# Scores of rounded units: the two heads of a pair in two halves of TensorE's rows, and queries rounded in one pass

## The chip, the cores and the metric

One core of a Trainium2 chip runs the kernel; seven stay idle. The metric is device time in microseconds of one execution, as the median of several runs. PE is TensorE (its weight loads are listed apart as PEld), DVE is VectorE, ACT ScalarE, POOL GpSimd, SP the engine that issues the DMAs.

## The reference

```python
B, H, S, D = 4, 8, 768, 48
for t in range(S):                       # a linear attention with decay, per head
    cur = u * kt (outer) vt
    y[:, :, t] = rt . (state + cur)
    state = wt * state + kt (outer) vt
x = y as (B * S, H * D) = (3072, 384)
x = elu(x @ w_in) @ w_out                # 384 -> 2048 -> 384
x = silu(x @ w2_in) @ w2_out             # 384 -> 2048 -> 384
```

All inputs and the output are float32.

## The kernel before

The attention is cut into 24 units: unit n is a chunk of L = 128 tokens of one batch (chunk n // 4, batch n % 4) with all 8 heads, as NP = 4 pairs. A pair lies in 112 partitions: its first head in rows 0 to 47 (padded to 64), its second in rows 64 to 111 (`HALF` names the two parts). For a unit, decays are built by scans on DVE, queries `tq` and keys `tk` are scaled with them, and within the chunk the output is a masked product of scores and values (`within`), outside of it a product with the state (`past`); `outer` and `update` bring the state on.

Scores are computed in one of two ways. Units 0 to 8 use plain float32: for each pair and head a matmul of the 64 or 48 rows of that head with 128 moving columns; the program issues each plain matmul as two passes, and the trace shows both. Units 9 to 23 (`n >= FIRST_ROUNDED`) use rounded float32: keys and queries are split into a high and a low part (`rounding`, lines 232 and 233: ACT copies to the rounded type, POOL subtracts), and three products, high by high, high by low, low by high, are added up in PSUM. There the queries are kept padded, `[112, 4, 2, 128]`, the first head's values in one of the two slots and zeros in the other rows (memset once, line 100), so that one matmul of all 112 rows and 256 moving columns gives the scores of both heads. A unit's scores come in two runs of six matmuls, `scores(0)` for pairs 0 and 1 and `scores(1)` for pairs 2 and 3, each into a PSUM bank of its own.

The two MLPs run in blocks of 512 tokens with all weights split in the same way into rounded high and low parts. A step f of the first MLP is `hidden` (line 443: nine matmuls of 512 columns), the activation (lines 450 to 459 on ACT and DVE), the split of its result (465 and 466) and, two steps later, `out_first` (line 474: nine matmuls). The second MLP is at lines 443 and 482.

The order is written out by hand. Units 0 to 3 run densely at the start; units 4 to 23 are threaded into the first MLP of the blocks before them. `slot` calls `tick` twice in each step f, once after `hidden` and once after `out_first`, and a tick takes the next of a unit's six parts (`round_ticks`). For unit n, with the preparation of unit n + 1 between its parts: t0 `scores(0)`, scan; t1 `scores(1)`, backward scan, `masked(0)`; t2 `masked(1)`, rounding of the queries of n + 1; t3 rounding of its keys; t4 nothing more for rounded units; t5 `past`, `outer`, `within` (lines 342, 316, 361), `ktok` of n + 1 (line 253: the keys transposed on PE, into the PSUM tile ktp), `update` (326, 328, 330), `split` (373, 374) and `ktok_copy` (line 259: ACT copies ktp away). Each engine works through its own instructions in the order of the program. In a block about four of five ticks take a part, so that between t5 and the next unit's t0 there are one or more groups of nine dense matmuls.

The PSUM tiles of scores, `ktp`, `upd`, `y` and the sums of unrounded units share one pool of three banks (`ps_a`). A tile that is allocated takes a bank that was used before, and its first writer waits until the last reader of that bank is done. `masked` (line 304) copies the scores above the diagonal on DVE into the attention tile `am`.

Of the kernel before, what the change touches and what calls it, by code (L numbers as in the profile page):

```python
# [7 lines left out]
F32 = mybir.dt.float32  # L8
F32R = mybir.dt.float32r
# [11 lines left out]
FIRST_ROUNDED = sum(BLOCKS[:2]) + 1  # L21
# [13 lines left out]
def kernel(  # L35
# [21 lines left out]
    nc = tc.nc  # L57
# [3 lines left out]
    RB = w_ch.shape[2]  # L61
    L = 128
    NCH = S // L
    NU = B * NCH
    NP = H // 2
# [24 lines left out]
    def rounded_open():  # L90
        staging.close()
        stage["x"] = attn.enter_context(tc.tile_pool(name="o1", bufs=1))
        stage["rk"] = attn.enter_context(tc.tile_pool(name="tok_rk", bufs=1))
        load_unit(SUMMED, "kr")
        p = attn.enter_context(tc.tile_pool(name="rounded", bufs=1))
        for i in "hl":
            rounded["k" + i] = p.tile([RB, NP, L], F32R, name="k" + i)

            q = rounded["q" + i] = p.tile([RB, NP, 2, L], F32R, name="q" + i)
            nc.gpsimd.memset(q.bitcast(F32), 0.0)  # L100

    x2_d = dram.tile([128, KT, NT], F32, name="x2_d")

# [2 lines left out]
    upper = const.tile([128, 128], I8, name="upper")  # L106
# [11 lines left out]
    rounded = {}  # L118
# [15 lines left out]
    HALF = (slice(0, 64), slice(64, RB))  # L134
# [5 lines left out]
    def load_unit(n, names):  # L140
        c, b = divmod(n, B)
        for nm in names if n < NU else "":
            if nm in "rk" and (n < SUMMED or "rk" not in stage):
                continue
            src, shape, pool, bufs = dict(
                w=(w_ch, [RB, W1 + 1], one_p, 2), c=(rk_ch, [RB, 2, NP, L], one_p, 2),
                r=(r_tok, [128, H * D], stage.get("rk"), 3), k=(k_tok, [128, H * D], stage.get("rk"), 3),
                v=(v_tok, [128, NP, 64 + D], tok_p, 2))[nm]
            t = un[n][nm] = pool.tile(shape, F32, tag="in_rk" if nm in "rk" else f"in_{nm}", name=f"in_{nm}", bufs=bufs)
            nc.sync.dma_start(t, src[b, c])  # L150

    def prep_steps(n):

        st = un[n]
# [76 lines left out]
        def rounding(x, hi, lo):  # L231
            nc.scalar.activation(out=hi, in_=x, func=ACTF.Copy)  # L232
            nc.gpsimd.tensor_tensor(out=lo, in0=x, in1=hi.bitcast(F32), op=ALU.subtract)  # L233

        def q():
            tq = st["q"] = ch_p.tile([RB, NP, L], F32, tag="tq", name="tq")
            nc.vector.tensor_tensor(out=tq, in0=st["c"][:, 0], in1=st["g4"][:, :, 0:L], op=ALU.mult)
            if n >= FIRST_ROUNDED:
                for e, rows in enumerate(HALF):
                    rounding(tq[rows], *(rounded["q" + i][rows, :, e, :] for i in "hl"))  # L240

        def kt():
            tk = st["kd"] = ch_p.tile([RB, NP, L], F32, tag="tk", name="tk")
# [11 lines left out]
        def ktok_copy():  # L255
            if n // B == NCH - 1:
# [3 lines left out]

        return dict(ktok=ktok, ktok_copy=ktok_copy, scan=scan, scan_back=scan_back, far=far, whole_decay=whole_decay, bonus=bonus, products=products, summed=summed, diag=diag,
                    q=q, kt=kt)


# [4 lines left out]
    def pe_steps(n, xt, col, free=None):  # L269
        ch, b = divmod(n, B)  # L270
        st = un[n]
        ps = {}

        def ps_att(shape, name):
            if free and name == "sc":
                return free.pop(0).rearrange("p (j t) -> p j t", j=NP)
            return ps_a.tile(shape, F32, tag="att", name=name)


        def scores(h):  # L280
            if n < FIRST_ROUNDED:

                if h == 0:
                    ps["p"] = [ps_att([128, NP, L], "sc") for _ in range(2)]
                for j in (2 * h, 2 * h + 1):
                    for e, rows in enumerate(HALF):
                        nc.tensor.matmul(
                            ps["p"][e][:, j, :], st["kd"][rows, j, :], st["q"][rows, j, :], start=True, stop=True)
                return
            p = ps["p", h] = ps_att([128, 2, 2, L], "sc")  # L290
            terms = [(rounded["k" + a], rounded["q" + b]) for a, b in ("hh", "hl", "lh")]
            for jj in range(2):
                j = 2 * h + jj
                for i, (a, b) in enumerate(terms):
                    nc.tensor.matmul(  # L295
                        p[:, jj].rearrange("p e t -> p (e t)"), a[:, j, :],
                        b[:, j].rearrange("p e t -> p (e t)"), start=i == 0, stop=i == len(terms) - 1)

        def masked(h):
            if n < FIRST_ROUNDED:  # L300
                to, p = st["a"][:, :, h, :], ps["p"][h]
            else:
                to, p = (t.rearrange("p j e t -> p (j e) t") for t in (st["a"][:, 2 * h:2 * h + 2], ps["p", h]))
            nc.vector.copy_predicated(to, upper.unsqueeze(1).to_broadcast([128, NP, L]), p)  # L304

        last = ch == NCH - 1

        def outer():
            if last:
                return  # L310
            p = ps["u"] = ps_att([RB, NP, D], "upd")
            for j in range(NP):

                for c in range(0, RB, 32):
                    rows, e = slice(c, min(c + 32, RB)), c // 64
                    nc.tensor.matmul(  # L316
                        p[rows, j, :], st["kt"][:, j, rows], st["v"][:, j, 64 * e:64 * e + D],
                        start=True, stop=True)

        def update():  # L320
            if last:
                return
            s, up = packed[b], ps["u"]
            g = st["gl"].to_broadcast([RB, NP, D])
            if ch:
                nc.vector.tensor_tensor(out=s, in0=up, in1=s, op=ALU.add)
                up = s
            nc.vector.tensor_tensor(out=s, in0=up, in1=g, op=ALU.mult)
            for e, rows in enumerate(HEAD):
                nc.scalar.activation(out=state[b][rows, :, e * D:(e + 1) * D], in_=s[rows], func=ACTF.Copy)  # L330

        def past():

            y = ps["y"] = ps_att([128, KT, L], "y")
            if not ch:
                return
            for kt in range(KT):
                for base in range(4):  # L340
                    j, i = divmod(4 * kt + base, 3)
                    nc.tensor.matmul(  # L342
                        y[32 * base:32 * base + 32, kt, :], state[b][:, j, 32 * i:32 * i + 32], st["q"][:, j, :],
                        start=kt == 0, stop=False, skip_group_check=True)

        def within():
            y = ps["y"]
            vf = st["v"].rearrange("p j c -> p (j c)")
            for step in range(4):
                for base in range(4):  # L350


                    todo = []
                    for kt in range(KT):
                        blk = 4 * kt + base
                        j, i = divmod(blk, 3)
                        ha, hb = (64 + D) * j, (64 + D) * j + 64
                        todo += {0: [(blk, 2 * j, ha)], 1: [(blk, 2 * j, ha + 32), (blk, 2 * j + 1, hb - 16)],
                                 2: [(blk, 2 * j + 1, hb + 16)]}[i]
                    blk, h, c = todo[step]  # L360
                    nc.tensor.matmul(  # L361
                        y[32 * base:32 * base + 32, blk // 4, :], vf[:, c:c + 32], st["a"][:, h // 2, h % 2, :],
                        start=not ch and step == 0, stop=step == 3 or todo[step + 1][0] != blk,
                        skip_group_check=True)

        def split():
            split_x(xt, slice(col, col + L), ps["y"], nc.vector)

        return dict(scores=scores, masked=masked, outer=outer,
                    update=update, past=past, within=within, split=split)  # L370

    def split_x(xt, sl, src, eng):
        nc.scalar.activation(out=xt["h"][:, :, sl], in_=src, func=ACTF.Copy)
        eng.tensor_tensor(
            out=xt["l"][:, :, sl], in0=src, in1=xt["h"].bitcast(F32)[:, :, sl], op=ALU.subtract)
# [356 lines left out]
    with tc.manual_schedule():  # L732
# [25 lines left out]
        for j, units in enumerate(BLOCKS):  # L758
# [38 lines left out]
            if j == 0:  # L797
                assert not halves and not whole
                rounded_open()
# [192 lines left out]
```

## Time and profile before

| | us |
|---|---|
| median of 3 runs (lowest, highest) | 949.76 (948.05, 950.05) |
| the profiled execution | 947.38 |
| its span on the core | 945.6 |
| PE busy in the span | 918.1 |
| DVE, ACT, POOL busy | 489.4, 502.4, 133.9 |

The profile is of one execution, which is not one of the three runs of the median. Busy shares are averages; what counts for a stage is which engine the others wait for in it. The duration that a matmul has in the trace is modelled and overlaps the next one, so distances between the starts of matmuls tell more than their durations. In a row of the timeline the numbers are the start in microseconds from the start of the span and the duration.

### The profile page before, as it was taken

To read this page: it belongs to the slowest core of one execution; us is meant where nothing else is said; L and a number is where in the kernel's file an instruction comes from. 1 tells how busy PE (TensorE), PEld (TensorE's weight loads), DVE (VectorE), ACT (ScalarE), POOL (GpSimd) and SP (SyncE) were. 2 spreads that over 40 slices of the span, in tenths; PEclk is the share of its full clock that TensorE was granted. 3 is DMA by queue.
4 is the path that set the end of the run, shared out by engine and by line. 5 is a ranking of instruction groups with operands and counts; after the bars stand their busy time and mean duration, and the time that the engine had idled before them with its cause. 6 is when DMAs were issued, how large, how long until landed. Compare 5 with 4: busy or idle time off the path is not lost.

```text
span 945.6 us, 15205 instructions
## 1 busy us (share of the span) xinstructions
PE 918.1 (97%) x6158; PEld 790.8 (84%) x6158; DVE 489.4 (52%) x726; ACT 502.4 (53%) x901; POOL 133.9 (14%) x101
## 2 busy tenths in 40 slices
PE   7779899999999999999999999999999999999996
PEld 7667688888888888888888899999999999999996
DVE  7798877776666776666378762212212212222211
ACT  6788866665655655555488963323323333333332
POOL 0000012443453334453000000000000000000000
PEclk8799999999999999999999999999999999999998
DMA  8644414222322221220245330100200200200001
GB/s 252 184 153 161 163 48 124 69 67 57 110 67 73 91 66 57 78 68 1 101 141 193 136 99 1 67 0 1 68 1 1 68 1 1 67 1 1 34 1 37
DMA packets 32222, 68.69 MB, mean 73 GB/s; under 512 B 3600, under 2 KB 13968, under 8 KB 32144
## 3 DMA queue, kind: packets, MB, share of 16 engines
q1 hardware_dynamic: 32144, 67.64, 22.5%
q8 instruction: 50, 0.82, 0.4%
q14 instruction: 28, 0.23, 0.1%
HBM read 58.19 MB, written 9.44 MB: 72 GB/s over the span
## 4 chain that ended last, share of the span: by engine, by line
PE 89%; DVE 6%; DMA 2%; ACT 2%; issue 1%; SPq 0%; DVEq 0%; ACTq 0%
PE ph L443 40%; PE po L482 21%; PE po L474 19%; PE sc L295 2%; PE y L361 2%; PE y L342 1%; DVE wst L414 1%; PE ktp L253 1%; DVE wl L429 1%; DVE wst L416 1%; DMA in_v<-in_v_tok_dram 1%; DVE am L304 1%; DVE gl L466 1%; PE upd L316 1%; DMA above_sb<-in_above_dram 1%
## 5 line engine op out<-in xcount | busy, mean ns | idle before, releaser
L466 DVE TENSOR_TENSOR gl<-g,gh 128x512 fp32r<-128x512 f32 x192 | 144.8, 754 | 313.5 <-ACT gh L465 313.3
L443 PE MATMUL ph<-xh,wh 128*128 128x512 f32 x576 | 227.6, 395 | 2.1 <-DVE g L459 2.1
L443 PE MATMUL ph<-xh,wl 128*128 128x512 f32 x576 | 227.4, 395 | 0.0
L443 PE MATMUL ph<-xl,wh 128*128 128x512 f32 x576 | 227.2, 394 | 0.0
L465 ACT ACTIVATE gh<-g 128x512 fp32r<-128x512 f32 x192 | 120.8, 629 | 153.7 <-PE po L482 109.7
L454 ACT ACTIVATE g<-ph 128x512 f32<-128x512 f32 x96 | 57.4, 598 | 137.8 <-PE ph L443 137.1
L482 PE MATMUL po<-wh,gl 128*128 128x384 f32 x384 | 129.5, 337 | 0.0
L482 PE MATMUL po<-wh,gh 128*128 128x384 f32 x384 | 129.3, 337 | 0.0
L482 PE MATMUL po<-wl,gh 128*128 128x384 f32 x384 | 128.9, 336 | 0.0
L443 PEld LDWEIGHTS ph<-xh,wl 128*128 128x128 f32 x576 | 108.7, 189 | 23.5
L443 PEld LDWEIGHTS ph<-xh,wh 128*128 128x128 f32 x576 | 109.1, 189 | 22.4 <-DVE g L459 2.5
L443 PEld LDWEIGHTS ph<-xl,wh 128*128 128x128 f32 x576 | 108.8, 189 | 19.5
L474 PE MATMUL po<-gh,wh 128*128 128x512 f32 x288 | 114.7, 398 | 0.0
L474 PE MATMUL po<-gl,wh 128*128 128x512 f32 x288 | 113.0, 392 | 0.0
L474 PE MATMUL po<-gh,wl 128*128 128x512 f32 x288 | 112.7, 391 | 0.0
L450 ACT ACTIVATE g<-ph 128x512 f32<-128x512 f32 x96 | 56.5, 589 | 52.2 <-PE ph L443 52.1
L459 DVE SCALAR_TENSOR_TENSOR g<-g,ph 128x512 f32<-128x512 f32 x96 | 65.4, 681 | 27.7 <-ACT g L452 27.1
L482 PEld LDWEIGHTS po<-wh,gh 128*128 128x128 f32 x384 | 72.2, 188 | 4.3 <-ACT x2s L493 0.2
L482 PEld LDWEIGHTS po<-wl,gh 128*128 128x128 f32 x384 | 72.1, 188 | 4.1
L482 PEld LDWEIGHTS po<-wh,gl 128*128 128x128 f32 x384 | 72.0, 188 | 0.0
L233 POOL TENSOR_TENSOR ql<-tq,qh 64x512 fp32r<-64x512 f32 (+1 forms) x30 | 42.7, 1423 | 167.1 <-ACT qh L232 166.0
L474 PEld LDWEIGHTS po<-gh,wh 128*128 128x128 f32 x288 | 54.5, 189 | 11.8 <-issue 0.8
(92 smaller groups left out, 1078.6 us busy)
## 6 DMA issues: line engine op xcount, KB each, us to landing
wst<-in_moe_w_in_dram SPq DMA_DIRECT2D x32, 384.0 KB, 3.2
wst<-in_moe_w_out_dram SPq DMA_DIRECT2D x32, 384.0 KB, 4.0
in_c<-in_rk_ch_dram SPq DMA_DIRECT2D x24, 448.0 KB, 3.8
in_w<-in_w_ch_dram SPq DMA_DIRECT2D x24, 226.2 KB, 2.7
in_v<-in_v_tok_dram SPq DMA_DIRECT2D x24, 224.0 KB, 3.1
x_d<-x2s SPq DMA_DIRECT2D x18, 256.0 KB, 2.4
xl<-x_d SPq DMA_DIRECT2D x6, 768.0 KB, 5.3
out_dram<-os SPq DMA_DIRECT2D x24, 192.0 KB, 2.0
```

The costliest lines, as they stand in the source:

```text
L233: nc.gpsimd.tensor_tensor(out=lo, in0=x, in1=hi.bitcast(F32), op=ALU.subtract)
L253: nc.tensor.transpose(p[:, j, :], st["kd"][:, j, :], ident[0:RB, 0:RB])
L295: nc.tensor.matmul(p[:, jj].rearrange("p e t -> p (e t)"), a[:, j, :], b[:, j].rearrange("p e t -> p (e t)"), start=i == 0, stop=i == len( ...
L361: nc.tensor.matmul(y[32 * base:32 * base + 32, blk // 4, :], vf[:, c:c + 32], st["a"][:, h // 2, h % 2, :], start=not ch and step == 0, st ...
L443: nc.tensor.matmul(ph, lhs, xt[rhs][:, kt, 0:nt], start=n == 0, stop=n == 3 * KT - 1)
L450: nc.scalar.activation(out=g, in_=ph, func=ACTF.Exp)
L454: nc.scalar.activation(out=g, in_=ph, func=ACTF.Silu)
L459: nc.vector.scalar_tensor_tensor(out=g, in0=g, scalar=-1.0, in1=ph, op0=ALU.mult, op1=ALU.max)
L465: nc.scalar.activation(out=gh, in_=g, func=ACTF.Copy)
L466: nc.vector.tensor_tensor(out=gl, in0=g, in1=gh.bitcast(F32), op=ALU.subtract)
L474: nc.tensor.matmul(po[ot][:, 0:nt], lhs, rhs, start=f == 0 and i == 0, stop=f == NF - 1 and i == 2)
L482: nc.tensor.matmul(po[t][:, 0:DM], lhs[:, sl], rhs["o", f], start=f == 0 and i == 0, stop=f == NF - 1 and i == 2)
```

## The change

In units 9 to 23 the queries are no longer padded: the high and the low part are tiles `[112, 4, 128]` like those of the keys, and each is made by one instruction over all 112 rows. The memsets of line 100 go away. The scores of a rounded unit are computed as those of the plain ones are, one matmul for each head in that head's rows, with 128 moving columns and each head's scores in a PSUM bank of its own; each of the three products of a pair is issued for the first head and then for the second. All 24 matmuls stand in `scores(0)`, which allocates both banks; `scores(1)` is empty. `masked` has one form for all units.

```diff
         for i in "hl":
-            rounded["k" + i] = p.tile([RB, NP, L], F32R, name="k" + i)
-
-            q = rounded["q" + i] = p.tile([RB, NP, 2, L], F32R, name="q" + i)
-            nc.gpsimd.memset(q.bitcast(F32), 0.0)
+            for x in "qk":
+                rounded[x + i] = p.tile([RB, NP, L], F32R, name=x + i)
...
             if n >= FIRST_ROUNDED:
-                for e, rows in enumerate(HALF):
-                    rounding(tq[rows], *(rounded["q" + i][rows, :, e, :] for i in "hl"))
+                rounding(tq, rounded["qh"], rounded["ql"])
...
         def scores(h):
+
+            if h == 0:
+                ps["p"] = [ps_att([128, NP, L], "sc") for _ in range(2)]
             if n < FIRST_ROUNDED:
-
-                if h == 0:
-                    ps["p"] = [ps_att([128, NP, L], "sc") for _ in range(2)]
-                for j in (2 * h, 2 * h + 1):
+                terms, pairs = [(st["kd"], st["q"])], (2 * h, 2 * h + 1)
+            else:
+                terms = [(rounded["k" + a], rounded["q" + b]) for a, b in ("hh", "hl", "lh")]
+                pairs = () if h else range(NP)
+            for j in pairs:
+                for i, (a, b) in enumerate(terms):
                     for e, rows in enumerate(HALF):
                         nc.tensor.matmul(
-                            ps["p"][e][:, j, :], st["kd"][rows, j, :], st["q"][rows, j, :], start=True, stop=True)
-                return
-            p = ps["p", h] = ps_att([128, 2, 2, L], "sc")
-            terms = [(rounded["k" + a], rounded["q" + b]) for a, b in ("hh", "hl", "lh")]
-            for jj in range(2):
-                j = 2 * h + jj
-                for i, (a, b) in enumerate(terms):
-                    nc.tensor.matmul(
-                        p[:, jj].rearrange("p e t -> p (e t)"), a[:, j, :],
-                        b[:, j].rearrange("p e t -> p (e t)"), start=i == 0, stop=i == len(terms) - 1)
+                            ps["p"][e][:, j, :], a[rows, j, :], b[rows, j, :],
+                            start=i == 0, stop=i == len(terms) - 1)

         def masked(h):
-            if n < FIRST_ROUNDED:
-                to, p = st["a"][:, :, h, :], ps["p"][h]
-            else:
-                to, p = (t.rearrange("p j e t -> p (j e) t") for t in (st["a"][:, 2 * h:2 * h + 2], ps["p", h]))
-            nc.vector.copy_predicated(to, upper.unsqueeze(1).to_broadcast([128, NP, L]), p)
+            nc.vector.copy_predicated(
+                st["a"][:, :, h, :], upper.unsqueeze(1).to_broadcast([128, NP, L]), ps["p"][h])
```

## Rows read from the trace of the kernel before

**Rows 1.** The page: busy time of the engines; the chain that ended last

```profile
PE 918.1 (97%) x6158; PEld 790.8 (84%) x6158; DVE 489.4 (52%) x726; ACT 502.4 (53%) x901; POOL 133.9 (14%) x101
...
PE 89%; DVE 6%; DMA 2%; ACT 2%; issue 1%; SPq 0%; DVEq 0%; ACTq 0%
```

**Rows 2.** Waits of PEld, 163 to 462 us: total, times, longest

```profile
PEld y L342 <- issue: 5.3, 15, 0.4
```

**Rows 3.** Timeline of PE, a rounded unit: start, duration, what, idle before and releaser

```profile
167.39 0.39 PE L474 MATMUL po<-gh,wl 128*128 128x512 f32 x1
167.62 0.28 PE L295 MATMUL sc<-qh,kh 112*128 112x256 f32 x1
...
168.34 0.40 PE L443 MATMUL ph<-xh,wh 128*128 128x512 f32 x1
...
170.41 0.28 PE L295 MATMUL sc<-qh,kh 112*128 112x256 f32 x1
...
173.19 0.39 PE L443 MATMUL ph<-xh,wh 128*128 128x512 f32 x1
...
175.23 0.39 PE L474 MATMUL po<-gh,wh 128*128 128x512 f32 x1
```

**Rows 4.** Timeline of PE, second half of an unrounded unit's scores

```profile
77.07 0.40 PE L474 MATMUL po<-gh,wl 128*128 128x512 f32 x1
77.39 0.72 PE L287 MATMUL sc<-tq,tk 64*128 64x128 f32 x8
78.04 0.50 PE L443 MATMUL ph<-xh,wh 128*128 128x512 f32 x1
78.38 0.39 PE L443 MATMUL ph<-xl,wh 128*128 128x512 f32 x1
...
80.21 0.95 PE L229 MATMUL sums<-u_ch,am 112*128 112x2 f32 x8
81.03 0.48 PE L474 MATMUL po<-gh,wh 128*128 128x512 f32 x1
```

**Rows 5.** Timeline of PE, an unrounded unit's scores in one run

```profile
51.74 1.16 PE L287 MATMUL sc<-tq,tk 64*128 64x128 f32 x16 [3.46 <-DVE tk L244]
52.83 0.98 PE L253 MATMUL ktp<-ident,tk 112*128 112x112 f32 x4
```

**Rows 6.** Timeline, first half of another unrounded unit's scores

```profile
115.48 0.49 PE L287 MATMUL sc<-tq,tk 64*128 64x128 f32 x2
...
116.63 0.54 ACT L259 ACTIVATE kt<-ktp 128x448 f32<-128x448 f32 x1
...
117.22 0.71 PE L287 MATMUL sc<-tq,tk 48*128 48x128 f32 x6 [1.25 <-ACT kt L259]
```

**Rows 7.** Timeline, ktok_copy and the start of the scores in two rounded units

```profile
245.19 0.28 PE L295 MATMUL sc<-qh,kh 112*128 112x256 f32 x1
245.31 0.54 ACT L259 ACTIVATE kt<-ktp 128x448 f32<-128x448 f32 x1
...
282.71 0.54 ACT L259 ACTIVATE kt<-ktp 128x448 f32<-128x448 f32 x1
...
283.98 0.28 PE L295 MATMUL sc<-qh,kh 112*128 112x256 f32 x1
```

**Rows 8.** Groups by line and shape, rounding: busy us, mean ns, idle before, releaser

```profile
L233 POOL TENSOR_TENSOR kl<-tk,kh 112x512 fp32r<-112x512 f32 x15 | 24.3, 1617 | 0.0
L233 POOL TENSOR_TENSOR ql<-tq,qh 48x512 fp32r<-48x512 f32 x15 | 22.9, 1528 | 1.1
...
L233 POOL TENSOR_TENSOR ql<-tq,qh 64x512 fp32r<-64x512 f32 x15 | 19.8, 1318 | 166.0 <-ACT qh L232 166.0
...
L232 ACT ACTIVATE kh<-tk 112x512 fp32r<-112x512 f32 x15 | 9.5, 633 | 11.1 <-DVE tk L244 10.9
L232 ACT ACTIVATE qh<-tq 48x512 fp32r<-48x512 f32 x15 | 9.4, 628 | 0.4
L232 ACT ACTIVATE qh<-tq 64x512 fp32r<-64x512 f32 x15 | 9.4, 625 | 8.1 <-DVE tq L237 8.1
```

## The prediction

> **What bounds the kernel now.** I read the page first, then the waits of the stretch that the change touches, then single instructions there in order of time. The page [rows 1]: PE is busy 97% of the 945.6 us, and the chain that ended last is 89% PE. So the time is a sum over PE's own instruction stream, and another engine counts only where PE is seen waiting for it. The change touches units 9 to 23, whose scores (line 295) run between 163 and 462 us. In that stretch PE itself is listed with no wait at all, and its weight loads with little [rows 2]: the largest entry is 5.3 us over 15 places, 0.35 us at each entry into the small matmuls of line 342, and it is put down to nothing outside PE. It comes back below as the price of a change of tiling. So each nanosecond that a score run gains or loses on PE is a nanosecond of the end.
>
> How long does a run last? A matmul's own duration is modelled and overlaps the next, so I use distances between starts. Away from scores a 512-column matmul follows the last one after 2.04/9 = 0.227 us (173.19 to 175.23, nine steps) [rows 3]. From the last dense matmul before a rounded run (167.39) to the first matmul of the next run (170.41) are 3.02 us; ten dense matmuls lie in it, 2.27 us, and 0.75 us are left for the run and its wake. A rounded unit has two such runs: **1.51 us**. No step of it is longer than the rest: six matmuls of 256 columns at 0.12 us (167.62 to 168.34), and the dense ones before and behind keep their pace.
>
> **The score run after the change.** Four pairs times three products times two heads are 24 matmuls in 12 steps of two, one in rows 0 to 63 and one in rows 64 to 111 of the array. No rounded matmul with 128 moving columns stands in the trace, and none in half the rows. The nearest rows are the scores of the unrounded units (line 287): the same two row halves, the same 128 columns, but plain float32, of which each matmul shows as two passes. Eight passes, four steps of two, cost by the same reckoning 80.21 - 77.07 = 3.14 us, less ten dense matmuls, **0.87 us** [rows 4]. What of this is steps and what is fixed? A run of 16 passes takes 1.09 us to the next matmul (51.74 to 52.83) [rows 5], one of 8 passes 0.65 us (77.39 to 78.04) [rows 4]: four more steps cost 0.44 us, 0.11 us each. So 0.44 us of the 0.87 are steps, and **0.43 us are fixed**: the run starts 0.32 us behind the dense matmul, not 0.23 (0.09 us to empty the array), its first step waits for weights that could not be loaded ahead, and the way back costs the same again; the dense matmul behind it needs 0.34 us (78.04 to 78.38), 0.11 us more than its pace, which is one weight load that nothing covers.
>
> The Trainium skill, "TensorEngine Tiling (Array Packing)", section Key Properties, says that a change of tiling mode drains TensorE. Of the fixed 0.43 us a drain on the way in and one on the way out would be 2 x 0.09 = 0.18 us; the rows show as much again for weight loads that lose their cover. By the drain alone a unit would cost, as an estimate from that page, 1.50 us, which is what it costs now (rival 2).
>
> What sets a step? The eight passes of line 229 move only 2 columns each and still take 0.82 us, 0.10 us each (80.21 to 81.03) [rows 4]. So the step follows the loading of 128 columns of weights, not the columns that move. The exposed 0.11 us behind the run are the load of a rounded weight in a full array, so rounded weights are no cheaper, and the two halves' loads already run side by side in the 0.11 us of [rows 5]. From below, a step limited by columns alone: 512 columns take 0.227 us and 256 take 0.12, so 128 would take 0.067 [rows 3]. From above, the two halves one after the other, or each rounded matmul run as two passes like a plain one: 0.22 us. Between: the 0.12 us of the rounded matmul as it is. I take 0.11, since the weight load is the row that both nearest cases obey.
>
> A unit then costs 0.43 + 12 x 0.11 = 1.75 us against 1.51: +0.24 to 0.25 us, over 15 units **+3.7 us**. At 0.12 a step it is +5.5 us. If the last matmul of a run leaves the array 0.04 us sooner because a rounded one of 128 columns streams in 0.067 us, it is 0.6 us less, +3.1 us.
>
> **A wait that comes with it.** Before, a rounded run takes one PSUM bank of the pool of three, and the second run takes the next one tick later (2.8 us later: 167.62 and 170.41 [rows 3]). After, both banks are taken at tick t0. The unrounded units do this already, and the trace shows what the second one waits for: at 115.48 us the two passes of the first half start, and the second half follows only at 117.22, released by ACT's copy of line 259 (ktok_copy, the last step of t5), which began at 116.63 and took 0.54 us [rows 6]. So the second bank is the one that ktp held. In the rounded stretch that copy is done 0.73 us or more before t0 in nine of the eleven units that have one (closest: copy ends 283.25, run starts 283.98 [rows 7]); in the last four units there is no ktp. In two units t0 comes only one group of dense matmuls behind t5: the run starts at 245.19 and the copy ends at 245.31 + 0.54 = 245.85 [rows 7], and one other unit repeats this pattern to the hundredth. The second half then waits for 245.90 instead of about 245.29, 0.6 us with the whole PE queue behind it: the rest of the run, the hidden matmuls of the next tile and all that ACT and DVE make of them. Twice, **+1.2 us**. If the second bank is another one of the pool, the wait is nothing or some tenths longer; I keep 0 to 1.6 us for the range.
>
> **What moves off PE.** Rounding of the queries was two ACT copies (0.625 and 0.628 us) and two POOL subtractions (1.32 and 1.53 us) a unit, one for each half of the rows; it becomes one copy and one subtraction of 112 rows, as the keys have them: 0.633 and 1.62 us [rows 8]. Over 15 units ACT gets 9.3 us back and POOL 18.4 us. I cost that at nothing: PE waits for neither in this stretch [rows 2], and the products are needed at t0 of the next unit, many microseconds later. Were that cover gone, ACT's share would be at most 0.6 us a unit. The memsets of the padded queries leave POOL, which has nothing behind them to hurry for. The mask copies (line 304) keep their number and shape, 2 of 128x512 a unit, and take the layout that they have in unrounded units; what they read is now complete one tick earlier. Six matmuls move from t1 to t0, past one group of dense matmuls, which nobody else waits for with PE in order; no DMA and no queue of SP moves.
>
> **Sum.** 3.7 + 1.2 = +4.9 us. The profiled execution took 947.38 us (span 945.6 and 1.8 around it) and would take 952.3; it lies 2.4 us under the median of the runs, 949.76. Against that median: **954.7 us**. With the bounds that I hold possible inside this case (step 0.11 to 0.12, last matmul shorter or not, wait 0 to 1.6): 952.9 to 956.9.
>
> **Rivals.** 1. The steps get cheaper than their weight loads (the change wins). If in half arrays rounded weights load behind the columns and a step is 0.067 us, a unit is 0.43 - 0.04 + 12 x 0.067 = 1.19 us, -0.32 x 15 = -4.8, with the wait 946.2 us. It decides below 0.09 us a step, where 0.43 + 12 x 0.09 = 1.51. For it: half the columns move. Against it: 2 columns take as long as 128. The Trainium skill, the same page, section Theoretical Speedup, gives up to 2x for a contraction of at most 64 rows; by that rule, an estimate, the products alone would fall from 1.51 to 0.75 us and with the fixed 0.43 us the time to about 945. The trace has no run that gains so: its row halves run side by side and still need 0.11 us. Chance 0.07.
> 2. The fixed cost is paid only in part, because one run of twelve steps lets PE load ahead what four steps don't, or only the two emptyings of 0.09 us are paid, and the copy of line 259 comes in time: from 2 x 0.09 + 12 x 0.11 = 1.50 to some 1.57 us a unit, 0 to +1 us, 950.2 in the middle. Against it: every change of tiling in the stretch shows the same gaps. Chance 0.12.
> 3. The halves don't run side by side for rounded data, or a rounded matmul this narrow falls back to two passes: 0.43 + 12 x 0.22 = 3.07 us, +1.56 x 15 = +23.4, with the wait 974. For it: no row shows one. Against it: 256 columns take 0.12 us and not twice that [rows 3], and plain passes do run side by side. Chance 0.08.
> The forecast keeps 0.73.
>
> **Chances and range.** A difference under about 0.2%, 1.9 us, can't be told from none. Slower by more: the forecast and rival 3, 0.81, less a little for its lower edge: 0.80. Faster by more: rival 1 and a rest, 0.08. Within: rival 2, 0.12. The range takes the forecast with its bounds and rival 2, and about a microsecond of scatter above: 950.2 to 958.0; rivals 1 and 3 stay outside.
>
> **What would show it.** Right: in the timeline of PE one run of 24 matmuls a unit, steps of 0.11 us from pair to pair, about 0.32 us before the first and 0.34 us behind the first dense one; two waits of PE on line 259; ACT and POOL lighter by 9 and 18 us, and no gain from it. Wrong: steps near 0.067 (rival 1), near 0.22 (rival 3), a dense pace that is not broken around the run (rival 2), or PE waits on another engine that stand nowhere before.

## The result and the profile after

The changed kernel takes 953.9 us (median, 953.34 to 956.22) against 949.76 us before; the ratio of the two is 1.0053 with a 95% interval of 1.0039 to 1.0066. It is slower: the medians are 4.1 us apart, and by the ratio it is 5.0 us. The page of its profile has a span of 952.1 us; its lines on the engines and on the chain, to hold against [rows 1]:

```profile
PE 925.4 (97%) x6338; PEld 791.7 (83%) x6338; DVE 504.7 (53%) x726; ACT 491.6 (52%) x886; POOL 104.8 (11%) x84
...
PE 82%; DVE 11%; ACT 3%; issue 2%; ACTq 0%; DVEq 0%
```

PE has 180 matmuls more (12 a unit in 15 units) and 7 us more of busy time. ACT lost 11 us and POOL 29 us, DVE gained 15 us although it has the same 726 instructions; that is the first sign of something that the prediction left out. DVE and ACT also take a larger part of the chain than before.

Where do the microseconds sit? The profiled executions differ by 6.5 us in their spans, and 1.9 of these lie ahead of the first unit that the change touches: the dense group at 163.42 us in the trace of before starts at 165.32 in the trace of after. Behind the last touched unit the groups at 466.72 and 473.63 answer each other, 6.9 us apart. So the stretch of the rounded units became **5.0 us** longer, and the rest is the start of the kernel, where the granted clock changes between full and half and does so at other moments in each execution (a half-speed stretch ends at 42.7 us in the trace of before and at 44.3 in that of after). The forecast had 4.9 for the stretch.

One rounded unit after, where nothing is waited for, is a timeline of PE (start, duration, what) to hold against [rows 3, 4]; "x2" is a step, one matmul in each half of the rows:

```profile
249.42 0.39 PE L465 MATMUL po<-gh,wl 128*128 128x512 f32 x1
249.74 0.33 PE L289 MATMUL sc<-qh,kh 64*128 64x128 f32 x2
249.90 0.28 PE L289 MATMUL sc<-ql,kh 64*128 64x128 f32 x2
250.01 0.28 PE L289 MATMUL sc<-qh,kl 64*128 64x128 f32 x2
...
251.02 0.28 PE L289 MATMUL sc<-qh,kl 64*128 64x128 f32 x2
251.22 0.49 PE L434 MATMUL ph<-xh,wh 128*128 128x512 f32 x1
251.56 0.39 PE L434 MATMUL ph<-xl,wh 128*128 128x512 f32 x1
```

The run starts 0.32 us behind the dense matmul, its first step takes 0.16 us, the ten others up to the last start (249.90 to 251.02) 0.11 each; 0.20 us later comes the next dense matmul, and that one needs 0.34 instead of 0.23. Reckoned as in the prediction, with everything up to nine dense matmuls behind it, a unit costs 1.72 us; the two runs of before cost 1.50 by the same reckoning with the trace's full resolution. That is +0.22 us, over 15 units **+3.3 us**.

The other 1.7 us are waits of PE in the middle of three runs, those of units 9, 10 and 11: 0.63, 0.41 and 0.61 us more than the 1.72, 1.65 in all. Unit 10, all engines:

```profile
179.86 3.22 DVE L457 TENSOR_TENSOR gl<-g,gh 128x512 fp32r<-128x512 f32 x1 [0.81 <-ACT gh L456]
180.64 1.90 POOL L207 TENSOR_TENSOR am<-ident,dg 128x1024 f32<-128x1024 f32 x1
...
186.63 0.79 DVE L319 TENSOR_TENSOR packed<-packed,whole 112x192 f32<-112x192 f32 x1
...
187.51 0.75 ACT L321 ACTIVATE state<-packed 48x192 f32<-48x192 f32 x2 [1.35 <-DVE packed L319]
...
188.68 0.54 ACT L256 ACTIVATE kt<-ktp 128x448 f32<-128x448 f32 x1
...
188.84 0.75 PE L289 MATMUL sc<-qh,kh 64*128 64x128 f32 x2
...
189.27 0.18 PEld L289 LDWEIGHTS sc<-qh,kh 48*128 48x128 f32 x1 [0.25 <-ACT kt L256]
```

The first half of the pair starts at 188.84; the second half loads its weights at 189.27, when the copy of ktp (188.68 + 0.54 = 189.22) has given its bank free. It is the wait of [rows 6], on the copy that the prediction named, but in other units than the two that it named.

The rounding did what was said of it; the groups of after answer [rows 8]:

```profile
L231 POOL TENSOR_TENSOR kl<-tk,kh 112x512 fp32r<-112x512 f32 x15 | 22.0, 1469 | 16.3 <-ACT kh L230 16.3
L231 POOL TENSOR_TENSOR ql<-tq,qh 112x512 fp32r<-112x512 f32 x15 | 20.1, 1343 | 178.1 <-ACT qh L230 178.1
...
L230 ACT ACTIVATE qh<-tq 112x512 fp32r<-112x512 f32 x15 | 9.4, 625 | 8.3 <-DVE tq L235 8.3
```

The queries' low parts took 42.7 us of POOL and take 20.1, the high parts 18.8 us of ACT and take 9.4.

### The profile page after: what moved, and what is told of

Same layout as the page of the kernel before. It is cut to its first block, busy times and chain, and to the rows that moved or that the text cites. A ratio compares the mean times of both kernels' runs of the same rounds, so it can differ in the third digit from the quotient of the medians.

```text
span 952.1 us, 15506 instructions
## 1 busy us (share of the span) xinstructions
PE 925.4 (97%) x6338; PEld 791.7 (83%) x6338; DVE 504.7 (53%) x726; ACT 491.6 (52%) x886; POOL 104.8 (11%) x84
## 4 chain that ended last, share of the span: by engine, by line
PE 82%; DVE 11%; ACT 3%; issue 2%; ACTq 0%; DVEq 0%
PE ph L434 37%; PE po L473 21%; PE po L465 17%; PE sc L289 2%; DVE gl L457 2%; PE y L352 2%; PE y L333 1%; DVE tk L241 1%; DVE am L294 1%; DVE both L158 1%; DVE wst L405 1%; DVE wst L407 1%; DVE g L450 1%; DVE wl L420 1%; ACT gh L456 1%
## 5 line engine op out<-in xcount | busy, mean ns | idle before, releaser
L457 DVE TENSOR_TENSOR gl<-g,gh 128x512 fp32r<-128x512 f32 x192 | 167.5, 872 | 302.3 <-ACT gh L456 302.0
L465 PEld LDWEIGHTS po<-gh,wl 128*128 128x128 f32 x288 | 54.3, 189 | 11.7
```

The source lines that it names most:

```text
L457: nc.vector.tensor_tensor(out=gl, in0=g, in1=gh.bitcast(F32), op=ALU.subtract)
L465: nc.tensor.matmul(po[ot][:, 0:nt], lhs, rhs, start=f == 0 and i == 0, stop=f == NF - 1 and i == 2)
```

## The experiments

The theory after the result: 3.3 us are the price of changing to the row halves and back once a unit, with a step that the weight load sets; 1.7 us are waits for the bank of ktp, and which units wait is decided by where POOL's work falls on DVE. The rivals: the loss sits in the steps themselves, or in putting the run together; and the waits belong to the longer run wherever POOL's work stands. Each kernel was timed beside the kernel before, and comparisons go by the ratio to it.

**early**: the copy of ktp at once behind its transposes.

```diff
             do("ktok")
+            do("ktok_copy")
             pe["update"]()
             pe["split"]()
-            do("ktok_copy")
```

> The changed kernel with ktok_copy placed right behind ktok, ahead of update and split, in t5 of every unit. Theory: part of the loss, about 1.7 us in units 9 to 11, is PE waiting at the first matmul of the second row half for the bank that this copy frees; with the copy no longer behind the state update on ACT, those three waits are gone (-1.7 us). The unrounded units 5 and 7 wait for the same copy already in the kernel before (2.2 and 1.7 us in the middle of their runs); if those go too it is -5.6 us in all: 948.3 to 952.2 us. Rival: the wait only moves on to the next late thing (the state update, which is now behind the copy, or the bank of upd), and the time stays at 953.9 within 0.5.

Measured: 947.93 us against 947.91 for the kernel before in the same series, ratio 0.9999 (0.9989 to 1.0009), where the changed kernel has 1.0053: about 5 us. All 15 rounded units cost 1.69 to 1.72 us, none waits. The timeline of unit 10, and of an unrounded unit that waited before [rows 6]:

```profile
181.48 0.53 ACT L256 ACTIVATE kt<-ktp 128x448 f32<-128x448 f32 x1
...
184.10 0.33 PE L289 MATMUL sc<-qh,kh 64*128 64x128 f32 x2
184.26 0.28 PE L289 MATMUL sc<-ql,kh 64*128 64x128 f32 x2
```

```profile
114.25 0.53 ACT L256 ACTIVATE kt<-ktp 128x448 f32<-128x448 f32 x1
...
115.08 0.71 PE L289 MATMUL sc<-tq,tk 64*128 64x128 f32 x8
```

The copy is done 2.1 us before the run in the first and 0.3 us before it in the second, whose eight passes now start together. So the waits are the copy's, in rounded and unrounded units. But the rival has a part: two waits of PE on DVE, which neither the kernel before nor the changed one has, stand in the dense matmuls and in the sums:

```profile
83.52 0.50 PE L465 MATMUL po<-gl,wh 128*128 128x512 f32 x1 [0.57 <-DVE gl L457]
...
99.25 1.05 PE L227 MATMUL sums<-u_ch,am 112*128 112x2 f32 x8 [0.85 <-DVE seed L157]
```

Against the trace of the changed kernel, from one dense group to the next, the three waits in rounded units make 1.7 us, the two in unrounded units 2.1 and 1.7 us, and a half-speed stretch of the clock at 75 us that is gone 1.2 us; the two new waits take back 1.1 us each.

**before_early**: the same move in the kernel before.

> The kernel before, with ktok_copy right behind ktok in t5, as in the run that did this to the changed kernel. Theory: that run came out level with the kernel before, 5.1 us under the changed kernel; 1.7 us of this are the three waits in rounded units and the rest, 2.9 to 3.9 us, the two waits on the same copy in unrounded units, which the kernel before has as well. So here -2.9 to -3.9 us: 945.9 to 946.9 against 949.8, ratio 0.996 to 0.997. Rival: the copy's place helps only where both banks are taken at t0 of rounded units; no change, ratio 1.000.

Measured: 944.1 us, ratio 0.9957 (0.9942 to 0.9972), 4.1 us less than before, against 2.9 to 3.9 expected. It beats both kernels. Its granted clock between 57 and 163 us is 1.00 where before has 0.97; the half-speed stretches of before there (3.4 us at 73.4 and 3.4 us at 107.5) are gone, and in the profiled execution the stretch from the dense group at 42 us to the one at 467 us is 3.4 us shorter. From one dense group to the next the two can be told apart. Of the waits, the one at 72.94 us is gone (1.9 us), the one at 117.22 gives way to a wait of 0.97 us on the state update (0.5 us less), and two on DVE are new, as in early (1.1 us each): together nothing. The two half-speed stretches that are gone make 1.4 and 1.5 us. So in the profiled executions the gain is nearly all the clock, not the waits that the theory priced; the size came out for another reason. Whether the other executions gained in the same way no trace shows.

**q_halves**: the queries rounded in two passes again, without the padding.

```diff
-                rounding(tq, rounded["qh"], rounded["ql"])
+                for rows in HALF:
+                    rounding(tq[rows], rounded["qh"][rows], rounded["ql"][rows])
```

> The changed kernel, but the queries are rounded in two passes again, one for each half of the rows, without the padding. Theory: which units wait for the bank is decided by where POOL's work falls beside DVE's split of line 457; with POOL as busy as before, units 9 to 11 no longer wait and units 13 and 17 wait 0.6 us each, 1.2 us in place of 1.7: 953.4 us, ACT +9 us, POOL +18 us or more. Rival: the waits of units 9 to 11 come with the longer run itself and stay where they are; 953.9 us and the same three waits in the trace.

Measured: 953.02 us, ratio 1.0062 (1.0043 to 1.0082), not to be told from the changed kernel. But the waits went where the prediction had put them: units 9 to 11 cost 1.72 us, unit 13 costs 2.33 and unit 17 costs 2.33, 0.61 us more each. Unit 13:

```profile
246.90 0.32 PE L290 MATMUL sc<-qh,kh 64*128 64x128 f32 x1
246.93 0.54 ACT L257 ACTIVATE kt<-ktp 128x448 f32<-128x448 f32 x1
247.52 0.32 PE L290 MATMUL sc<-qh,kh 48*128 48x128 f32 x1 [0.30 <-ACT kt L257]
```

So with two copies and two subtractions a unit, as before, the forecast of the wait holds to 0.01 us and by unit, and it is the shorter rounding that moved it.

**pool_halves**: one ACT copy, two POOL subtractions.

```diff
-                rounding(tq, rounded["qh"], rounded["ql"])
+                nc.scalar.activation(out=rounded["qh"], in_=tq, func=ACTF.Copy)
+                for rows in HALF:
+                    nc.gpsimd.tensor_tensor(
+                        out=rounded["ql"][rows], in0=tq[rows], in1=rounded["qh"][rows].bitcast(F32), op=ALU.subtract)
```

> The changed kernel with one ACT copy for the queries' high part, but two POOL subtractions for the low part, one for each half of the rows. Theory: the place of POOL's 128x1024 product (line 207) beside DVE's split of line 457 decides which units wait; with POOL's work as before the change, units 9 to 11 don't wait for the copy of ktp and units 13 and 17 do, about 0.6 us each. Rival: ACT's saved copy is what moved the waits; then units 9 to 11 wait as in the changed kernel, three times 0.4 to 0.65 us.

Measured in one execution: 949.97 us. Neither came: no unit waits at all, all cost 1.69 to 1.72 us, and the stretch of the rounded units is 3.4 us longer than before, which is 15 x 0.22 and nothing else. For units 9 to 11 it is POOL's work that decides, as the theory had it, since only POOL differs from the changed kernel here. For units 13 and 17 it is ACT's copy, since only ACT differs from q_halves; that POOL's work alone decides was wrong. The traces show how the copy acts, ahead of unit 13 first in q_halves, then in pool_halves:

```profile
239.99 1.90 POOL L207 TENSOR_TENSOR am<-ident,dg 128x1024 f32<-128x1024 f32 x1
240.01 2.42 DVE L458 TENSOR_TENSOR gl<-g,gh 128x512 fp32r<-128x512 f32 x1 [2.62 <-ACT gh L457]
```

```profile
238.26 1.38 DVE L460 TENSOR_TENSOR gl<-g,gh 128x512 fp32r<-128x512 f32 x1 [1.69 <-ACT gh L459]
...
239.17 2.23 POOL L207 TENSOR_TENSOR am<-ident,dg 128x1024 f32<-128x1024 f32 x1
```

DVE's split waits for ACT's copy of the high part, which stands behind the queries' copies. With two of them the split starts 0.02 us behind the start of POOL's product and takes 2.42 us; with one it starts 0.9 us ahead of it and takes 1.38. Unit 17 is the same (323.18 and 323.20 us in q_halves). So the place of the product beside the split decides there too, and ACT moves the split.

**two_runs**: the 24 matmuls in two runs again.

```diff
-                pairs = () if h else range(NP)
+                pairs = (2 * h, 2 * h + 1)
```

> The changed kernel, but the scores of a rounded unit are issued in two runs again, pairs 0 and 1 at t0 and pairs 2 and 3 at t1, still one head in each half of the rows. Theory: a change of tiling to the row halves and back costs 0.39 us whatever the run's length; a second one for each of 15 units adds 5.9 us: 959.8 us (959 to 960.5). Rival: the loss sits in the steps of the run, and cutting it in two changes nothing: 953.9 us; or the fixed cost is only a drain of 0.09 us each way: +2.7 us, 956.6 us.

Measured: 958.23 us, ratio 1.0107 (1.0087 to 1.0127), 5.1 us above the changed kernel by the ratios. One run of six steps:

```profile
235.13 0.39 PE L465 MATMUL po<-gh,wl 128*128 128x512 f32 x1
235.45 0.33 PE L289 MATMUL sc<-qh,kh 64*128 64x128 f32 x2
...
236.06 0.28 PE L289 MATMUL sc<-qh,kl 64*128 64x128 f32 x2
236.27 0.50 PE L434 MATMUL ph<-xh,wh 128*128 128x512 f32 x1
236.61 0.39 PE L434 MATMUL ph<-xl,wh 128*128 128x512 f32 x1
```

The same 0.32, 0.20 and 0.34 us stand around a run of half the length. Six steps cost 1.02 us and twelve 1.72: so 0.32 us are fixed and 0.70/6 = 0.117 is a step. The price is paid for each change to the halves and back, and more than the two drains of 0.09 us; but 0.32, not 0.39 or 0.43. It is the trace that tells this: the intervals of the two ratios leave 2 to 8 us between the kernels. The profiled stretch of the rounded units is 4.0 us longer than in the changed kernel, 15 x 0.32 = 4.8 less 0.8, since the waits of units 9 to 11 shrink to 0.8 us in all.

**padded_one_run**: the padded matmuls of before, all twelve at t0.

```diff
-            p = ps["p", h] = ps_att([128, 2, 2, L], "sc")
+            if h:
+                return
+            for g in range(2):
+                ps["p", g] = ps_att([128, 2, 2, L], "sc")
...
-            for jj in range(2):
-                j = 2 * h + jj
+            for j in range(NP):
+                p, jj = ps["p", j // 2], j % 2
```

> The kernel before with its padded queries and full-array matmuls, but all twelve of a unit issued at t0 into both banks (nothing at t1). Theory: one run alone costs nothing, since no tiling changes; the wake behind a run, 0.03 us, is paid once and not twice, and the second bank is needed only behind the first six matmuls (0.72 us), which covers the copy that frees it: 949.3 us (948.8 to 949.8). Rival: putting the run together and taking both banks at t0 is itself what costs, by the wait for the second bank: 951.0 to 951.5 us.

Measured: 949.47 us, ratio 1.0007 (0.9995 to 1.0019), no difference. A unit costs 1.47 us in one run against 1.50 in two, and units 13 and 17 wait 0.09 us each instead of 0.6, since the second bank is needed six matmuls later. So one run for a unit is free in itself; the row halves are what costs.

**narrow_full**: twelve matmuls of all 112 rows with 128 moving columns. It adds the scores of the two heads of a pair into one bank and masks both heads from the sum.

```diff
-                ps["p"] = [ps_att([128, NP, L], "sc") for _ in range(2)]
+                ps["p"] = [ps_att([128, NP, L], "sc") for _ in range(2 if n < FIRST_ROUNDED else 1)]
...
-                    for e, rows in enumerate(HALF):
+                    for e, rows in enumerate(HALF if n < FIRST_ROUNDED else [slice(0, RB)]):
...
-                st["a"][:, :, h, :], upper.unsqueeze(1).to_broadcast([128, NP, L]), ps["p"][h])
+                st["a"][:, :, h, :], upper.unsqueeze(1).to_broadcast([128, NP, L]), ps["p"][h if n < FIRST_ROUNDED else 0])
```

> The changed kernel with twelve rounded matmuls a unit, all 112 rows by 128 moving columns in the full array, into one bank; the scores of the two heads of a pair are summed and not kept apart, both masks read the sum. So it has the narrow matmul without the change of tiling and without a second bank. Theory: a step is set by the weight load, 0.11 us in a full array as in the halves: 12 x 0.11 + 0.03 = 1.35 to 1.40 us a unit against 1.50 before, -1.5 to -2.2 us: ratio to the kernel before 0.9975 to 0.9985. Rival: columns set the step, 0.067 us: 0.83 us a unit, -10 us, ratio 0.989; or a narrow rounded matmul runs as two passes, 0.22 us: +18 us, ratio 1.019.

Measured: 952.94 us, ratio 1.0041 (1.0024 to 1.0057), slower and not 0.2% faster. The run itself is as the theory has it:

```profile
230.12 0.39 PE L434 MATMUL ph<-xh,wl 128*128 128x512 f32 x1
230.35 0.22 PE L289 MATMUL sc<-qh,kh 112*128 112x128 f32 x1
...
231.53 0.28 PE L289 MATMUL sc<-qh,kl 112*128 112x128 f32 x1
231.64 0.44 PE L465 MATMUL po<-gh,wh 128*128 128x512 f32 x1
```

No gap ahead of it, steps of 0.11 us with half the columns of before, 1.39 us a unit: -0.11 us, -1.6 us in all. The step of 128 columns is neither 0.067 nor 0.22. Against the changed kernel it also prices the halves alone: 1.724 - 1.388 = 0.34 us for the same twelve steps. The stretch of the rounded units is 3.4 us longer than before all the same. Most of the loss is in one place: from the dense group at 280.5 us to the next at 288.8 it is 3.8 us longer than before. Two shorter waits of PE, for the keys that DVE makes (0.53 us at 184.5, 0.67 us at 221.7), add 1.3 us: -1.6 + 3.8 + 1.3 makes nearly the 3.4. The timeline at the long one (all engines), and the granted clock of three stretches (each engine's busy time and instructions, then PEclk):

```profile
279.59 3.22 DVE L457 TENSOR_TENSOR gl<-g,gh 128x512 fp32r<-128x512 f32 x1 [0.82 <-ACT gh L456]
280.37 1.89 POOL L207 TENSOR_TENSOR am<-ident,dg 128x1024 f32<-128x1024 f32 x1
...
282.87 0.65 PE L465 MATMUL po<-gl,wh 128*128 128x512 f32 x1 [1.94 <-DVE gl L457]
```

```profile
276.00:282.80 6.80, 4.93 (x22) 3.75 (x20) 5.98 (x7) 3.37 (x6) 3.15 (x2) 1.00 0.13 34
283.10:286.50 3.40, 3.40 (x12) 2.17 (x15) 2.64 (x4) 2.34 (x4) 1.28 (x1) 0.50 0.48 135
286.60:300.00 13.40, 13.40 (x147) 11.49 (x140) 8.60 (x17) 6.69 (x14) 2.03 (x2) 1.00 0.22 65
```

DVE's split of line 457 needs 3.22 us, PE waits 1.94 us for it, and behind the wait the granted clock is at 1.2 GHz for 3.4 us, which makes about the other 1.8 us. A second half-speed stretch lies at 119 us, before the first rounded unit; it costs 1.5 us and has nothing to do with the edit. The edit's own share of the measured time is therefore not told by the ratio.

**halves_apart**: all twelve matmuls of the first head, then all twelve of the second.

```diff
+            todo = [(j, i, e) for j in pairs for i in range(len(terms)) for e in range(2)]
+            if n >= FIRST_ROUNDED:
+                todo.sort(key=lambda t: t[2])
+            for j, i, e in todo:
...
```

> The changed kernel with the 24 matmuls of a rounded unit in another order: all twelve of the first head, then all twelve of the second, so that neighbours share their rows. Theory: the two halves' loads and columns run side by side only between neighbours in different rows; apart, 24 steps of 0.11 us, 2.64 + 0.35 = 3.0 us a unit against 1.72, +19 us, while the waits for the second bank vanish behind the first twelve (-1.7): 971 us. Rival: PE looks far enough ahead to run the second half beside the first, or each matmul is limited by its columns: 0.067 x 24 + 0.35 = 1.96 us a unit, +3.6 - 1.7 us: 956 us.

Measured in one execution: 968.58 us. The run of one unit:

```profile
231.47 0.32 PE L291 MATMUL sc<-qh,kh 64*128 64x128 f32 x1
231.63 0.27 PE L291 MATMUL sc<-ql,kh 64*128 64x128 f32 x1
...
232.41 0.27 PE L291 MATMUL sc<-qh,kl 64*128 64x128 f32 x1
232.42 0.38 PE L291 MATMUL sc<-qh,kh 48*128 48x128 f32 x2
232.58 0.33 PE L291 MATMUL sc<-ql,kh 48*128 48x128 f32 x2
232.70 0.32 PE L291 MATMUL sc<-qh,kl 48*128 48x128 f32 x2
232.81 0.27 PE L291 MATMUL sc<-qh,kh 48*128 48x128 f32 x1
...
233.70 0.27 PE L291 MATMUL sc<-qh,kl 48*128 48x128 f32 x1
233.90 0.50 PE L467 MATMUL po<-gh,wh 128*128 128x512 f32 x1
```

It takes 2.67 us, between the two forecasts: matmuls in the same half follow each other at 0.11 us, and only where the second half begins are three of its matmuls side by side with the last three of the first: 21 steps of 0.11 and the fixed 0.33 are 2.64. The wait for the bank is gone. Twice in the stretch, at 276.0 and at 467.1 us, the clock stood at half speed for 3.4 us, both times behind such a run; that is 3.3 us more of the 20.9 by which the stretch grew against before.

## Why the prediction was right, step by step

**PE is the sum.** Right. In the traces of after, early, before_early, q_halves, pool_halves and narrow_full, set against that of before from one dense group to the next, every difference over 0.3 us in the stretch is a run's length, a wait of PE that the trace names, or the clock.

**The run.** Right in mechanism and nearly in size: 1.75 us forecast, 1.72 found. Its two parts were off against each other: the fixed cost is 0.32 us (two_runs) to 0.34 (narrow_full), not 0.43, and a step costs 0.117, not 0.11: 0.111 from start to start, and the dense matmuls behind the longer run are a little slower. The 0.43 came from plain float32 runs [rows 4, 5], whose first step takes 0.21 us; a rounded one takes 0.16. The prediction had seen that a rounded matmul leaves the array sooner and had kept the 0.04 us for its range instead of the sum. +3.7 forecast, +3.3 found.

**The step follows the weight load.** Right as far as the runs go: half the columns in the full array gave 0.11 us a step (narrow_full), so the columns of a rounded matmul don't set it, and PEld's loads there follow each other without a gap at 0.111 to 0.112 us. The passes of 2 columns do the same (0.112 from start to start; the prediction's 0.10 is a mean with a shorter first step). The plain scores that the prediction leaned on as well prove less: in the kernel before, plain passes with only 32 columns of weights, four side by side, take 0.109 us a step at 128 moving columns (line 361) and 0.042 at 48 (line 316), so a plain pass of 128 columns needs 0.11 us by its columns too, and there the two can't be told apart. The same rows, with starts 0.006 us apart, speak against a fixed price of 0.11 us for every matmul. No run changed the number of weight columns alone. That is why the change can't win: before, 256 columns stream in about the time in which 128 columns of weights load; halving the columns leaves the load, and the second head beside the first only wins back what the padding had cost.

**The wait for ktp's bank.** Right in kind and, with 1.65 us against 1.2, nearly in size; wrong by unit. The total, +4.9 against +5.0, came nearer than either of its terms, which is luck. The step that failed is the next one.

**"I cost that at nothing."** This is what failed: the microseconds that ACT and POOL got back were reckoned as harmless because PE waits for neither. But a shorter queue also starts its next instruction sooner. Ahead of unit 10, DVE's split of an MLP step, 2.3 us before the products of t5 in both kernels, was not held up before. The timeline of DVE in the kernel before:

```profile
177.10 0.69 DVE L466 TENSOR_TENSOR gl<-g,gh 128x512 fp32r<-128x512 f32 x1 [1.63 <-ACT gh L465]
177.71 1.79 DVE L244 TENSOR_TENSOR tk<-in_c,both 112x512 f32<-112x512 f32 x1
```

There POOL's second subtraction, from 177.20 on, held the next operation a little (1.79 us). After, the same split started at 179.86, behind the start of POOL's single subtraction (179.38 to 180.68), and ended 0.5 us behind POOL's next product (180.64 + 1.90 = 182.54): 3.22 us instead of 0.69. All that follows on DVE, and through the state update on ACT the copy of ktp, came late, in units 9 to 11; in units 13 and 17 the same shift brought the copy forward, from 0.66 us after the run's start to 0.82 before it. The Trainium skill, "SBUF — State Buffer", section "SBUF: two separate sides", says that DVE and GpSimd share a pair of ports, which one instruction holds until it is done while the other is blocked. The trace agrees in what it shows, 3.22 us against 0.69, and in that the split, with two operands in SBUF, ends behind POOL's work; which port is held no run shows. It is no single case: of the 192 splits of this kind 13 take over 2 us in the changed kernel, 3 in the kernel before and in q_halves, and none in pool_halves, and these splits alone took 22.6 us more of DVE than before, against the 15 us that DVE gained as a whole. The cost was +1.65 in place of +1.2 us, luck more than reckoning: pool_halves shows that the same change with another length of POOL's work has no wait at all, and against that the single subtraction costs 1.6 us (stretches 5.0 and 3.4 us longer than before).

**The rivals.** The step limited by columns (1) did not come, and narrow_full says why. The fixed cost in part (2) has a share of truth, 0.32 and not 0.43, but the whole 0.18 of two drains is too little. The halves one after the other (3) did not come; halves_apart shows that they run side by side when issued alternately and hardly else, and prices that at 0.95 us a unit.

Open: what makes the two new waits on DVE when the copy of ktp is moved up; whether the clock gives before_early its gain in every execution as it did in the profiled one; and, since pool_halves and halves_apart have one execution each, how far their times scatter.

## What to carry to other kernels

Splitting a short contraction into row halves does not pay where the loading of weights sets the step, as it did here at 0.11 us for 128 columns, and a kernel that mixes it with full-array matmuls pays about a third of a microsecond for each change there and back, so put as much as possible into one run. Ask of every instruction that is made shorter what its engine will start sooner and whom that meets: here the split of DVE met POOL's next product. And when a PSUM bank is waited for, look at who frees it and whether that reader stands behind work that it does not need: moving one copy up took the changed kernel back to the time of the kernel before (ratio 0.9999). But look at where such a gain sits: in the kernel before, the same move gained 4.1 us, and in its trace nearly all of that is the clock.

## What the runs showed of the hardware that was not expected

A DVE operation of 0.69 us took 3.22 us when it began behind a POOL operation, through two POOL operations in a row. A wait of PE of 1.94 us was followed by 3.4 us at the lower granted clock (0.50), so it cost nearly twice its length; runs of 2.4 us with one half of the rows busy at a time were followed by the same fall twice in fifteen. Not every wait of such a length was followed so: PE waited 2.06 us ahead of 107.05 us in the kernel before, with the clock at half from 107.5 on, and 2.12 us ahead of 106.91 in before_early, where it stayed full. And PE ran the last three matmuls of one row half side by side with the first three of the other, but not more.
